# Attention scores in two row tiles of the matmul array, unpadded queries, and a re-ordered opening in a fused attention and feed-forward kernel

## The chip, the cores and the metric

The kernel runs on one core of one Trainium2 chip. The metric is the device time of one execution in microseconds (us), taken as the median of several runs; lower is better. The core has five engines with a queue each that work side by side: PE (matmuls, with its weight loads shown as PEld), DVE (elementwise and reductions), ACT (activation functions and copies), POOL (small copies, and issuing DMAs that change the type) and SP (issuing the other DMAs). They wait for each other through semaphores.

## The reference

Eight batches of eight heads, 576 positions, 64 values a head. Attention sees a window of 32 positions to each side and 8 global positions, which see everything and are seen by all. Its output is the input of a two-layer feed-forward block.

```python
scores = scale * np.matmul(q, k.transpose(0, 1, 3, 2))
mask = np.abs(pos[:, None] - pos[None, :]) <= 32
mask = mask | is_global[:, None] | is_global[None, :]
scores = np.where(mask, scores, -1000000000.0)
scores = scores - np.max(scores, axis=-1, keepdims=True)
attn = np.exp(scores)
attn = attn / (np.sum(attn, axis=-1, keepdims=True) + 1e-09)
x = np.matmul(attn, v)              # to (4608, 512)
h = x @ w_in                        # (4608, 2048)
g = h * np.cos(h)
out = g @ w_out                     # (4608, 512)
```

## The kernel before

**Attention.** Work is cut into 32 pairs of heads (`pr`), four to a batch. For a pair the queries lie in 11 blocks of 56, and each block sees 120 keys of its window and the 8 global ones, 128 in all. The 8 global queries ride along with every block, so that a block has 64 columns (C). Per pair there are these steps:

- `local_k`, `local_q` fill `kw` (keys, two heads of 64 rows stacked on 128 partitions) and `qb` (queries). For the first eight pairs they transpose on PE (`turned`, L492); from then on they copy from `kT`, `qT`, which DMA transposes have filled. `globals_k`, `globals_q` put the global columns in, on POOL.
- `scores(pr, g)` (s): `qb` has a plane for each head in which the other head's 64 rows are zero. One matmul of 128 rows and 128 columns per block then gives both heads side by side. It is called three times a pair, for 4, 4 and 3 blocks; each call has one PSUM bank (tag "s", a ring of three), one exponential on ACT (L527) and one product with the mask on DVE (L528, into `pm`).
- `values(pr)` (p): 22 matmuls of 65 columns (64 values and the row sum) into `pv`, half-width tiles of the array, then sums, reciprocals and the scaled result `xn` on DVE (L542 to L548).
- `turn_x(pr)` (x): six transposes on PE and two DVE operations put `xn` into `xT`; after the last pair of a batch POOL copies the 8 global rows (L568).
- `spread(pr)` (w), for the first eight pairs only: builds `vw`, the values by windows, with 31 small matmuls against shift matrices (L370, L374). Later pairs load `vw` by DMA.

**Feed-forward.** `mlp_in` is a unit of four matmuls of 512 columns (L578), followed by a cosine on ACT (L584) and a product on DVE (L585). The cosine and the exponential need different tables on ACT, so a table load stands at each change. `mlp_out` is a unit of four matmuls of 512 columns (L595); four units fill one output tile, which ACT and DVE copy out in turn and SP stores. There are 144 units of either kind. First-layer units use the PSUM ring "h" (two banks), second-layer units the one bank "o"; while `spare` is on, half of the first-layer units use ring "s".

**Order.** The programmer writes the order by hand, and each engine works through its own part of it strictly in turn. `FRONT` lists the opening, pairs 0 to 7. Then come rounds `s` = 3 to 15. Round 3 (`MID`) has no attention but 18 first-layer units. Each later round has two pairs, called a and z, and follows a string: `1` is a first-layer unit, `2` a second-layer unit, `kc qc kd qd` prepare the next round's pairs, `n` is the sum of squares of `xn` on ACT, `G` issues casts on POOL, `bring` issues transposes and loads on SP. Rounds 4, 5 and 6 have strings of their own (`FOURTH`, `FIFTH`, `SIXTH`). A first-layer unit is only issued when its rows of `xT` are ready; where they are not, the place in the string stays empty. `FIFTH` is the round where only what is left of the first two row tiles can be issued. After the rounds the tail alternates the two kinds of units until all are done.

Of the kernel before, what the change touches and what calls it, by code (L numbers as in the profile page):

```python
# [9 lines left out]
FP32 = mybir.dt.float32  # L10
FP16 = mybir.dt.float16
I32 = mybir.dt.int32
AF = mybir.ActivationFunctionType
# [6 lines left out]
P = 128  # L20
# [24 lines left out]
FOURTH = "2 2 sa0 sa1 sa2 2 sz0 2 sz1 sz2 pa 1 1 2 xa pz G 1 1 2 xz n 1 1 2 kc qc 1 kd qd 2 1"  # L45

FIFTH = "sa0 sa1 sa2 2 2 2 sz0 2 sz1 sz2 pa 1 2 xa pz G 1 2 xz n 1 2 kc qc 1 kd qd 2"

SIXTH = "sa0 sa1 sa2 2 2 2 sz0 2 sz1 sz2 pa 1 1 2 xa pz G 1 1 2 xz n 1 1 D0 2 kc qc D1 1 kd qd D2 2 1"
# [149 lines left out]
def kernel(  # L199
# [138 lines left out]

    def hold(pr):

        nc.gpsimd.tensor_copy(gate, qb[pr % NK][0:1, 0, 0, G : G + 1])

    def vn16(s):
        return xT[:, s, 6 * TT : 9 * TT].rearrange("p (i n) -> p i n", i=NVT)
# [16 lines left out]
    def spread(pr):  # L361

        new, h0 = vn16(pr // 2), 2 * (pr % 2) * D
        for g0 in range(0, NB, 4):
            n = min(4, NB - g0)
            t = ps.tile([P, 4, P], FP32, tag="s", bufs=3)
            for j in range(g0, g0 + n):
                i = j // 2
                parts = ((2, i), (3, i + 1)) if j % 2 else ((0, i), (1, i - 1))
                nc.tensor.matmul(t[:, j - g0], own[:, pr], vg16[:, 0].rearrange("p h d -> p (h d)"), start=True, stop=False)  # L370
                parts = [(a, x) for a, x in parts if x >= 0]
                for a, x in parts:
                    m = min(VT, S - VT * x)
                    nc.tensor.matmul(t[:, j - g0], shift[0:m, a], new[0:m, x, h0 : h0 + 2 * D],  # L374
                                     start=False, stop=(a, x) == parts[-1])
            copy = nc.vector.tensor_copy if g0 == 4 else nc.scalar.copy
            copy(vw[pr % NV][:, g0 : g0 + n, :, 0:D], t[:, 0:n].rearrange("p n (h d) -> p n h d", h=2))

# [4 lines left out]
                view(vg16[(pr % 16) * G : (pr % 16 + 1) * G, pr // 16, h], (0, NB), (1, D)))  # L383


    mask = keep.tile([P, NB, 2, C], FP16)

    def build_mask():

        kid = work.tile([P, NB], FP32, tag="kid", bufs=1)  # L390
        nc.vector.tensor_copy(kid, kid_i)
        gf = work.tile([P, G], FP32, tag="gf", bufs=1)
        nc.vector.tensor_copy(gf, view(gidx_all, (2, G)))
        eq = work.tile([P, NB, G], FP32, tag="eq", bufs=1)
        nc.vector.tensor_tensor(eq, view(kid, (1, NB), (0, G)), view(gf, (0, NB), (1, G)), ALU.is_equal)
        isg = work.tile([P, NB], FP32, tag="isg", bufs=1)
        nc.vector.tensor_reduce(isg, eq, AX.X, ALU.max)
        ge0 = work.tile([P, NB], FP32, tag="ge0", bufs=1)
# [16 lines left out]
        for h in range(2):  # L415
            nc.vector.tensor_tensor(
                mask[:, :, h, G:], view(nk, (1, NB), (0, QB)), view(band[:, G:], (0, NB), (1, QB)), ALU.mult)
            nc.vector.tensor_scalar(
                mask[:, :, h, 0:G], view(val, (1, NB), (0, G)), own[:, 0:1], None, ALU.mult)
# [11 lines left out]
        for h in range(2):  # L431
            nc.vector.tensor_copy(mask[0:G, :, h, G:], view(one, (0, NB), (0, QB)))


    qgT = keep.tile([P, B * NP, G], FP16)
# [44 lines left out]

    def globals_q(pr):
        qp = qb[pr % NK]
        nc.gpsimd.tensor_copy(qp[0:D, 0, :, 0:G], view(qgT[0:D, pr], (0, NB), (1, G)))
        nc.gpsimd.tensor_copy(qp[D:P, 1, :, 0:G], view(qgT[D:P, pr], (0, NB), (1, G)))

    def turned(src, pr, n):

# [14 lines left out]
            nc.vector.tensor_copy(to, view(kT[pr // 2 % 2][:, pr % 2], (QB, NB), (1, W)))  # L502

    def local_q(pr):
        if pr < 2 * HY:
            t = turned(qn[pr // 2 % 2], pr, QP)
        for h in range(2):
            hp = slice(h * D, (h + 1) * D)
            to = qb[pr % NK][hp, h, :, G:]
            if pr < 2 * HY:  # L510
                copy = nc.scalar.copy if h == 0 or pr == 1 else nc.vector.tensor_copy
                copy(view(to, (C, NB), (RW, QB // RW), (1, RW)),  # L512
                     view(t[hp], (QB // RW, NB), (1, QB // RW), (QP, RW)))
            else:
                nc.vector.tensor_copy(to, view(qT[pr // 2 % 2][hp, pr % 2], (QB, NB), (1, QB)))  # L515

    def scores(pr, g):
        kp, qp = kw[pr % NK], qb[pr % NK]
        if g == 0:
            pm_of[pr] = work.tile([P, NB, 2, C], FP16, tag="pm", name="pm")  # L520
        pm = pm_of[pr]
        g0, n = 4 * g, min(4, NB - 4 * g)
        st = ps.tile([P, 4, P], FP32, tag="s", bufs=3)
        for j in range(n):
            nc.tensor.matmul(st[:, j], kp[:, g0 + j], view(qp[:, :, g0 + j], (NB * C, 2), (1, C)), start=True, stop=True)  # L525
        e = work.tile([P, 4, P], FP16, tag="e", bufs=3)
        nc.scalar.activation(e[:, :n], st[:, :n], AF.Exp, scale=scale)  # L527
        nc.vector.tensor_tensor(  # L528
            view(pm[:, g0], (1, n * P)), view(e, (1, n * P)), view(mask[:, g0], (1, n * P)), ALU.mult)

    def values(pr):
        pm, vp = pm_of.pop(pr), vw[pr % NV]
        for j in range(NB):
            for h in range(2):
                r0 = (j % 2) * C
                c0 = ((j // 2) % 3) * 130 + h * 65
                nc.tensor.matmul(pv[r0 : r0 + C, j // 6, c0 : c0 + 65], pm[:, j, h], vp[:, j, h],  # L537
                                 start=True, stop=True)
        den = pv[:, :, D : D + 1]
        rp = r_all[:, pr]  # L540
        dg = work.tile([G, 2], FP32, tag="dg")
# [10 lines left out]
    def turn_x(pr):  # L552
# [142 lines left out]
    with tc.manual_schedule():  # L695
# [14 lines left out]
        gather(k, kg32, 0)  # L710
        gather(q, qg32, 0)
        gather(v, vg32, 0)
        for t in (kn[1], qn[1], qb[2], qb[3]):
            nc.scalar.memzero(t.rearrange("p a b c -> p (a b c)"))
        load_qk(1)
        for i in range(2):
            nc.vector.memset(qb[i], 0.0)
        build_shifts()
        for i in range(NV):
            nc.vector.memset(vw[i][:, :, :, D : D + 1], 1.0)  # L720
# [53 lines left out]
                 "w": spread, "C": cast_vn, "V": lambda _: hold(9), "A": later_rows, "D": later_globals, "O": load_w_out, "K": lambda s: cast_half(s, "kq" if s == 4 else "vkq"), "B": bring, "m": lambda _: one(False), "t": lambda _: mlp_act()}  # L774
        ready[0] = 1
        for step in FRONT.split():
            f = (STEPS | OTHER)[step[0]]
            f(*[int(x) for x in (step[1:] or "0").split(".")])
        ready[0], front[0] = 2, False
# [85 lines left out]
```

## Time and profile before

| | us |
|---|---|
| median of 3 runs (367.13, 369.73, 370.02) | 369.73 |
| profiled execution | 371.58 |
| its span, first instruction to last | 369.8 |
| opening (`FRONT`), up to the first matmul of MID | 0 to 71.65 |
| MID, 18 first-layer units | 71.65 to 87.78 |
| rounds 4 to 15 | 87.78 to about 291 |
| tail | about 291 to 369.8 |

Costs of single operations, from the groups by line: exponential of 512 columns 596 ns, of 384 columns 492; mask product 427 and 361; cosine 687; product g 685; query copy on DVE 460 (a 64-partition plane, two to a pair), on ACT 667 and 803 on DVE in the opening; sum of squares 1476; table load 1283.

How to read it: a timeline row gives start, length, engine, line, operation and tiles, and how many like instructions were merged; what stands in brackets is the idle time before and what ended it. Matmuls overlap, and the end of each is modelled, so the time of one is read from start to start. "Issue" in the chain of waits is time in which the engine waited for nothing that the profile shows.

### The profile page before, as it was taken

What the parts mean: (1) busy time and instruction counts of PE and PEld (TensorE: products, weight loads), DVE (VectorE), ACT (ScalarE), POOL (GpSimd) and SP (SyncE); (2) the same over time, 40 slices, a digit from 0 to 9 for tenths busy, and PEclk for the clock granted to TensorE, in tenths of its full rate; (3) what the DMA queues carried; (4) which work ended last, traced back from release to release, by engine and by line L of the source; (5) the groups of instructions that cost most, each with busy time, mean ns of one, the idle gap of its engine ahead of it and who ended that gap; (6) DMA issues with size and microseconds to landing.
All of it is one profiled execution on the core that took longest, in us unless ns stands there. A gap on an engine that the chain in (4) does not pass through costs nothing.

```text
span 369.8 us, 8014 instructions
## 1 busy us (share of the span) xinstructions
PE 335.9 (91%) x2934; PEld 184.9 (50%) x2934; DVE 266.3 (72%) x615; ACT 249.5 (67%) x384; POOL 105.9 (29%) x239
## 2 busy tenths in 40 slices
PE   0399883999998999999999999999999999999992
PEld 0277673545553545555555555555555444444441
DVE  7659974696888888888888888888878445455410
ACT  5488882679776677778777868677787756644300
POOL 6735670161335250705253252603000100000000
PEclk9999997899999999999999999999999999999999
DMA  5979999999999999999999999999920000100111
GB/s 92 197 129 159 180 165 107 198 176 147 102 161 105 194 126 195 125 169 138 195 161 159 160 142 165 160 202 118 130 59 31 28 30 28 57 30 28 53 64 65
DMA packets 176280, 45.57 MB, mean 123 GB/s; under 512 B 164937, under 2 KB 171337, under 8 KB 176041
## 3 DMA queue, kind: packets, MB, share of 16 engines
q1 hardware_dynamic: 112601, 27.61, 58.3%
q0 software_dynamic: 63632, 17.37, 50.3%
q8 instruction: 25, 0.41, 0.5%
q14 instruction: 22, 0.18, 0.2%
HBM read 45.07 MB, written 20.05 MB: 176 GB/s over the span
## 4 chain that ended last, share of the span: by engine, by line
PE 79%; DVE 6%; issue 5%; ACT 3%; POOL 3%; DMA 2%; POOLq 0%; ACTq 0%
PE po L595 32%; PE ph L578 30%; PE st L525 5%; PE pv L537 4%; PE tx L560 2%; PE t L374 2%; DMA qn<-in_q_dram 2%; DVE g L585 2%; ACT e L527 1%; PE t L370 1%; PE t L492 1%; PE pn L628 1%; DVE xn L548 1%; POOL q L262 1%; ACT qb L512 1%
## 5 line engine op out<-in xcount | busy, mean ns | idle before, releaser
L584 ACT ACTIVATE cos<-ph,pio 128x512 f16<-128x512 f32 x144 | 97.1, 687 | 66.3 <-PE ph L578 64.7
L595 PE MATMUL po<-w_out,g 128*128 128x512 f16 x576 | 141.6, 379 | 0.0
L578 PE MATMUL ph<-xT,w_in 128*128 128x512 f16 x576 | 140.1, 379 | 0.3 <-DVE g L585 0.2
L585 DVE TENSOR_TENSOR g<-cos,ph 128x512 f16<-128x512 f16 x144 | 95.9, 685 | 46.9 <-ACT cos L584 44.9
L595 PEld LDWEIGHTS <-g 128*128 128x128 f16 x576 | 55.2, 98 | 62.1
L578 PEld LDWEIGHTS <-w_in 128*128 128x128 f16 x576 | 53.6, 98 | 60.5 <-issue 1.3
L527 ACT ACTIVATE e<-st 128x512 f16<-128x512 f32 (+1 forms) x96 | 47.9, 561 | 15.5 <-PE st L525 9.4
L528 DVE TENSOR_TENSOR pm<-e,mask 128x512 f16<-128x512 f16 (+1 forms) x96 | 37.2, 405 | 22.8 <-ACT e L527 21.0
L752 POOL COPY gate<-xn 1x1 f16<-1x1 f16 x12 | 2.2, 181 | 132.3 <-DVE xn L548 132.3
L525 PE MATMUL st<-qb,kw 128*128 128x128 f16 x352 | 29.2, 223 | 9.4 <-issue 5.0
L525 PEld LDWEIGHTS <-kw 128*128 128x128 f16 x352 | 24.1, 100 | 19.8 <-issue 9.1
L548 DVE TENSOR_TENSOR xn<-pv,r_all 128x768 f16<-128x768 f32 x32 | 30.7, 958 | 1.7
L568 POOL COPY xT<-xg 128x4 f16 x64 | 19.6, 306 | 28.7 <-DVE xT L563 25.3
L262 POOL DMA_DIRECT2D q<-in_q_dram x12 | 26.2, 2181 | 0.0
L614 ACT ACTIVATE sq<-xn 128x1536 f16<-128x1536 f16 x16 | 23.6, 1476 | 0.0
L515 DVE COPY qb<-qT 64x616 f16<-64x616 f16 x48 | 22.1, 460 | 0.3
L374 PE MATMUL t<-xT 112*128 112x128 f16 (+1 forms) x168 | 21.1, 240 | 0.7 <-ACT xT L349 0.4
L600 ACT COPY o<-po 128x512 f32<-128x512 f32 x18 | 10.5, 586 | 15.5 <-PE po L595 15.1
L262 POOL DMA_DIRECT2D k<-in_k_dram x12 | 19.8, 1646 | 0.0
L370 PE MATMUL t<-vg,xT 128*128 128x128 f16 x88 | 18.4, 242 | 0.9 <-issue 0.6
L537 PE MATMUL pv<-vw,pm 128*64 128x65 f16 x704 | 18.5, 199 | 0.0
L602 DVE COPY o<-po 128x512 f32<-128x512 f32 x18 | 12.3, 685 | 6.9 <-PE po L595 6.9
(123 smaller groups left out, 326.8 us busy)
## 6 DMA issues: line engine op xcount, KB each, us to landing
out_dram<-o SPq DMA_DIRECT2D x36, 256.0 KB
vw<-v SPq DMA_DIRECT2D x35, 165.0 KB
v<-in_v_dram POOLq DMA_DIRECT2D x12, 288.0 KB, 4.3
k<-in_k_dram POOLq DMA_DIRECT2D x12, 288.0 KB, 9.2
q<-in_q_dram POOLq DMA_DIRECT2D x12, 288.0 KB, 15.8
vn<-in_v_dram SPq DMA_DIRECT2D x20, 112.0 KB
w_in<-in_moe_w_in_dram POOLq DMA_DIRECT2D x4, 512.0 KB, 12.3
w_out<-in_moe_w_out_dram POOLq DMA_DIRECT2D x1, 2048.0 KB
```

What stands on the lines that cost most here:

```text
L262: nc.gpsimd.dma_start(dst[s].rearrange("t (h d) -> t h d", h=4), dview(src, base, (D, S), (S * D, 4), (1, D)))
L374: nc.tensor.matmul(t[:, j - g0], shift[0:m, a], new[0:m, x, h0 : h0 + 2 * D], start=False, stop=(a, x) == parts[-1])
L525: nc.tensor.matmul(st[:, j], kp[:, g0 + j], view(qp[:, :, g0 + j], (NB * C, 2), (1, C)), start=True, stop=True)
L527: nc.scalar.activation(e[:, :n], st[:, :n], AF.Exp, scale=scale)
L528: nc.vector.tensor_tensor(view(pm[:, g0], (1, n * P)), view(e, (1, n * P)), view(mask[:, g0], (1, n * P)), ALU.mult)
L537: nc.tensor.matmul(pv[r0 : r0 + C, j // 6, c0 : c0 + 65], pm[:, j, h], vp[:, j, h], start=True, stop=True)
L548: nc.vector.tensor_tensor(view(xn, (384, 2), (D, 6), (1, D)), view(pv, (512, 2), (65, 6), (1, D)), view(rp, (6, 2), (1, 6), (0, D)), ALU.mult)
L578: nc.tensor.matmul(ph, w_in16[:, j, f * P : (f + 1) * P], xT[:, j, t * TT : (t + 1) * TT], start=(j == 0), stop=(j == NC - 1))
L584: nc.scalar.activation(cos, ph, AF.Sin, bias=pio2)
L585: nc.vector.tensor_tensor(g, cos, ph, ALU.mult)
L595: nc.tensor.matmul(po, g16[:, f, s * P : (s + 1) * P], w_out16[:, f], start=(f == 0), stop=(f == NF - 1))
L614: nc.scalar.activation(sq, view(xn, (1, 2 * BP * P)), AF.Square, accum_out=x_sq[:, s : s + 1])
```

## The change

- `qb` loses its planes: both heads lie in one tile of 128 partitions without zeros. `local_q` is one copy, and in the opening it is on DVE for even pairs and on ACT for odd ones; `globals_q` is one copy. The clearing of `qb` goes, and the mask is kept once instead of per head.
- `scores(pr)` is one call. Each block has two matmuls, one per head, on 64 rows of the array; each head writes its own PSUM banks. Four banks are used at a time: three of ring "s", and one of "o" in the opening or of "h" in the rounds. Exponentials are two of 512 columns and two of 192; mask products are two of 512 columns and one of 384.
- `values` issues its matmuls so that the column halves alternate.
- `spread` merges neighbouring matmuls: 16 instead of 31 a pair.
- `turn_x` always uses ring "s".
- The orders: in a round the two score calls stand whole, with four second-layer units between them (`FOURTH`: two ahead and two between); eight second-layer units a round as before. In `FRONT` values and transposes come one stage later, four first-layer units are issued instead of two, with the spare banks on, and the second sum of squares closes it.

```diff
-ORDER = "sa0 sa1 sa2 2 2 2 sz0 2 sz1 sz2 pa 1 1 2 xa pz G 1 1 2 xz n 1 1 2 kc qc 1 kd qd 2 1"
+ORDER = "sa 2 2 2 2 sz pa 1 1 2 xa pz G 1 1 2 xz n 1 1 2 kc qc 1 kd qd 2 1"
...
-FIFTH = "sa0 sa1 sa2 2 2 2 sz0 2 sz1 sz2 pa 1 2 xa pz G 1 2 xz n 1 2 kc qc 1 kd qd 2"
+FIFTH = "sa 2 2 2 2 sz pa 1 2 xa pz G 1 2 xz n 1 2 kc qc 1 kd qd 2"
...
-FRONT = ("s0.0 s0.1 s0.2 k1 q1 C0 w0 s1.0 s1.1 s1.2 L2 p0 k2 q2 C1 w1 x0 s2.0 s2.1 s2.2 W0 p1 k3 q3 C2 w2 x1 "
-         "s3.0 s3.1 s3.2 L3 W1 A g4 g5 p2 k4 q4 w3 x2 s4.0 s4.1 s4.2 g6 g7 c4 K4 W2 W3 p3 k5 q5 C3 w4 x3 s5.0 s5.1 s5.2 p4 k6 q6 w5 x4 n0 "
-         "s6.0 s6.1 s6.2 K5 p5 k7 q7 w6 x5 B4 s7.0 s7.1 s7.2 O p6 w7 n1 x6 m p7 m x7 t t")
+FRONT = ("s0 k1 q1 C0 w0 s1 L2 k2 q2 C1 w1 p0 s2 W0 k3 q3 x0 C2 w2 p1 s3 L3 W1 A g4 g5 k4 q4 x1 w3 p2 "
+         "s4 g6 g7 c4 K4 W2 W3 k5 q5 x2 C3 w4 p3 s5 k6 q6 x3 w5 p4 s6 K5 k7 q7 x4 w6 p5 s7 B4 O w7 x5 n0 p6 + m m x6 p7 t t m m x7 t t n1 -")
...
-    qb = [keep.tile([P, 2, NB, C], FP16, name=f"qb{i}") for i in range(NK)]
+    qb = [keep.tile([P, NB, C], FP16, name=f"qb{i}") for i in range(NK)]
...
+            nc.tensor.matmul(view(t, (1, n * P)), own[:, pr], view(vg16[:, 0].rearrange("p h d -> p (h d)"), (0, n), (1, P)),
+                             start=True, stop=False, skip_group_check=True)
+            for a, j, k, x in runs:
+                m = min(VT, S - VT * x)
+                nc.tensor.matmul(view(t[:, j], (2 * P, k), (1, P)), shift[0:m, a], new[0:m, x : x + k, h0 : h0 + 2 * D],
+                                 start=False, stop=(a, j, k, x) == runs[-1], skip_group_check=True)
...
-    def scores(pr, g):
...
-        for j in range(n):
-            nc.tensor.matmul(st[:, j], kp[:, g0 + j], view(qp[:, :, g0 + j], (NB * C, 2), (1, C)), start=True, stop=True)
...
+    def scores(pr):
+        kp, qp = kw[pr % NK], qb[pr % NK]
+        pm = pm_of[pr] = work.tile([P, 2, NB, C], FP16, tag="pm", name="pm")
+        tags = (("s", 3), ("s", 3), ("s", 3), ("o", 1) if front[0] else ("h", 2))
+        st = [ps.tile([P, 512], FP32, tag=tag, bufs=bufs, name="st") for tag, bufs in tags]
+        for j in range(NB):
+            for h in range(2):
+                hp = slice(h * D, (h + 1) * D)
+                nc.tensor.matmul(st[j // 8 * 2 + h][:, j % 8 * C : j % 8 * C + C], kp[hp, j], qp[hp, j], start=True, stop=True)
         for h in range(2):
+            e = work.tile([P, 512], FP16, tag="e", bufs=3)
+            nc.scalar.activation(e, st[h], AF.Exp, scale=scale)
+            nc.vector.tensor_tensor(view(pm[:, h], (1, 512)), e, view(mask, (1, 512)), ALU.mult)
+        e = work.tile([P, 512], FP16, tag="e", bufs=3)
+        n = (NB - 8) * C
+        for h in range(2):
+            nc.scalar.activation(e[:, h * n : (h + 1) * n], st[2 + h][:, 0:n], AF.Exp, scale=scale)
+        nc.vector.tensor_tensor(view(pm[:, 0, 8], (NB * C, 2), (1, n)), view(e, (n, 2), (1, n)), view(mask[:, 8], (0, 2), (1, n)), ALU.mult)
...
-        for j in range(NB):
+        for j0 in range(0, NB, 2):
             for h in range(2):
...
+                for j in range(j0, min(j0 + 2, NB)):
...
-        tx = ps.tile([P, BP, P], FP16, tag="o" if front[0] else "s", bufs=1 if front[0] else 3)
+        tx = ps.tile([P, BP, P], FP16, tag="s", bufs=3)
...
-        for t in (kn[1], qn[1], qb[2], qb[3]):
+        for t in (kn[1], qn[1]):
...
-        for i in range(2):
-            nc.vector.memset(qb[i], 0.0)
```

More of the change, by code (lines that the diff above doesn't have):

```diff
@@ L366, in spread @@
             t = ps.tile([P, 4, P], FP32, tag="s", bufs=3)
[L367 to L375, printed above, removed]
+            runs = []
+            for first, a, back in ((0, 0, 0), (0, 1, 1), (1, 2, 0), (1, 3, -1)):
+                js = [j for j in range(g0 + first, g0 + n, 2) if j // 2 - back >= 0]
+                full = [j for j in js if j // 2 - back < NVT - 1]
+                runs += [(a, x[0] - g0, len(x), x[0] // 2 - back) for x in (full, js[len(full) :]) if x]
+            nc.tensor.matmul(view(t, (1, n * P)), own[:, pr], view(vg16[:, 0].rearrange("p h d -> p (h d)"), (0, n), (1, P)),
[4 more added lines that the diff above has]
+                                 start=False, stop=(a, j, k, x) == runs[-1], skip_group_check=True)
             copy = nc.vector.tensor_copy if g0 == 4 else nc.scalar.copy
@@ L383, in load_vg @@
                 view(vg16[(pr % 16) * G : (pr % 16 + 1) * G, pr // 16, h], (0, NB), (1, D)))
-    mask = keep.tile([P, NB, 2, C], FP16)
+    mask = keep.tile([P, NB, C], FP16)
     def build_mask():
@@ L414, in build_mask @@
         nc.vector.memset(own[0:G], 0.0)
[L415 to L419, printed above, removed]
+        nc.vector.tensor_tensor(
+            mask[:, :, G:], view(nk, (1, NB), (0, QB)), view(band[:, G:], (0, NB), (1, QB)), ALU.mult)
+        nc.vector.tensor_scalar(
+            mask[:, :, 0:G], view(val, (1, NB), (0, G)), own[:, 0:1], None, ALU.mult)
         gc = work.tile([G, 1], FP32, tag="gc", bufs=1)
@@ L430, in build_mask @@
         nc.vector.tensor_scalar(one, one, 0.5, None, ALU.is_le)
-        for h in range(2):
-            nc.vector.tensor_copy(mask[0:G, :, h, G:], view(one, (0, NB), (0, QB)))
+        nc.vector.tensor_copy(mask[0:G, :, G:], view(one, (0, NB), (0, QB)))
     qgT = keep.tile([P, B * NP, G], FP16)
@@ L504, in local_q @@
     def local_q(pr):
+        to = qb[pr % NK][:, :, G:]
         if pr < 2 * HY:
             t = turned(qn[pr // 2 % 2], pr, QP)
-        for h in range(2):
[L508 to L515, printed above, removed]
@@ L517, in scores @@
-    def scores(pr, g):
[L518 to L523, printed above, removed]
-        for j in range(n):
[L525 to L529, printed above, removed]
+            copy = nc.scalar.copy if pr % 2 else nc.vector.tensor_copy
@@ L531, in values @@
     def values(pr):
         pm, vp = pm_of.pop(pr), vw[pr % NV]
-        for j in range(NB):
+        for j0 in range(0, NB, 2):
             for h in range(2):
[L535 to L538, printed above, removed]
+                for j in range(j0, min(j0 + 2, NB)):
+                    r0 = (j % 2) * C
+                    c0 = ((j // 2) % 3) * 130 + h * 65
+                    nc.tensor.matmul(pv[r0 : r0 + C, j // 6, c0 : c0 + 65], pm[:, h, j], vp[:, j, h],
+                                     start=True, stop=True)
@@ L776 @@
         for step in FRONT.split():
+            if step in "+-":
+                spare[0] = step == "+"
+                continue
+            if step in "+-":
+                spare[0] = step == "+"
+                continue
             f = (STEPS | OTHER)[step[0]]
```

13 lines of the change are left out of this document (8 added, 5 removed).

## The prediction

> **What bounds it now.** I read the page first, then busy time by stage, then one late round engine by engine, then the opening and its chain of waits.
>
> ```profile
> PE 335.9 (91%) x2934; PEld 184.9 (50%) x2934; DVE 266.3 (72%) x615; ACT 249.5 (67%) x384; POOL 105.9 (29%) x239
> ```
>
> PE is busy 91%. By stage (columns: stretch, length, busy time of PE, weight loads, DVE, ACT, POOL, granted clock, DMA share, GB/s):
>
> ```profile
> 52.20:62.30 10.10, 4.02 (x84) 3.29 (x78) 4.54 (x11) 4.45 (x9) 1.72 (x2) 0.93 1.51 92
> 62.30:72.40 10.10, 9.43 (x108) 6.88 (x108) 5.86 (x17) 6.42 (x10) 0.00 (x0) 0.74 1.68 185
> 72.40:87.90 15.50, 15.27 (x71) 6.74 (x69) 13.82 (x26) 12.57 (x20) 8.62 (x24) 1.00 1.65 167
> 138.66:155.58 16.92, 16.92 (x143) 9.07 (x142) 14.22 (x33) 12.92 (x20) 6.19 (x14) 1.00 1.66 160
> ```
>
> So three regimes: an opening to 71.6 us with PE waiting; the block MID, 18 first-layer units one after the other; then rounds of 16.92 us in which PE has no gap while DVE idles 2.7 us and ACT 4.0 us. One round on PE:
>
> ```profile
> 154.80 0.78 PE L525 MATMUL st<-qb,kw 128*128 128x128 f16 x11
> 155.41 2.75 PE L595 MATMUL po<-w_out,g 128*128 128x512 f16 x12
> 158.00 0.39 PE L525 MATMUL st<-qb,kw 128*128 128x128 f16 x4
> 158.23 1.03 PE L595 MATMUL po<-w_out,g 128*128 128x512 f16 x4
> 159.09 0.55 PE L525 MATMUL st<-qb,kw 128*128 128x128 f16 x7
> 159.57 0.57 PE L537 MATMUL pv<-vw,pm 128*64 128x65 f16 x22
> 160.07 1.90 PE L578 MATMUL ph<-xT,w_in 128*128 128x512 f16 x8
> ```
>
> Read start to start: 11 score matmuls 0.61 us (55.5 ns each), a unit of four 512-column matmuls 0.864, seven scores ahead of the values 0.48 where 0.39 is due: going over to half-width tiles costs 0.09. The 22 value matmuls take 0.50, about 0.41 without the way back, so 18.6 ns each.
>
> ACT and DVE in the same round:
>
> ```profile
> 157.00 2.02 ACT L527 ACTIVATE e<-st 128x512 f16<-128x512 f32 x4
> 159.51 0.98 ACT L527 ACTIVATE e<-st 128x512 f16<-128x512 f32 x2 [0.49 <-DVE pm L528]
> 160.51 1.28 ACT L584 ACT_TABLE_LOAD   x1
> 161.80 1.27 ACT L584 ACTIVATE cos<-ph,pio 128x512 f16<-128x512 f32 x2
> ```
> ```profile
> 161.44 0.96 DVE L548 TENSOR_TENSOR xn<-pv,r_all 128x768 f16<-128x768 f32 x1
> 162.53 1.28 DVE L585 TENSOR_TENSOR g<-cos,ph 128x512 f16<-128x512 f16 x2
> ...
> 165.68 1.28 DVE L585 TENSOR_TENSOR g<-cos,ph 128x512 f16<-128x512 f16 x2
> ```
>
> ACT works strictly in turn: exponentials, table load, cosines; DVE follows it with pm, xn, then the products g.
>
> **The rounds.** Count from the first score matmul (154.80 = 0). Before: exponentials end at 5.69, the cosine table is loaded by 7.0, the first g starts on DVE at 7.73, xn of the first pair ends at 7.60, PE starts its transposes at 7.88, the fifth first-layer unit at 11.74 only 0.18 after the g (third of the round) that frees its bank. PE sets the pace with 0.2 to 0.3 us to spare.
>
> After, a score call is 22 matmuls of 64 rows and 64 columns, the heads alternating. No row shows row tiles. Nearest: the transposes of keys, which alternate between two column halves:
>
> ```profile
> 35.70 0.50 PE L492 MATMUL t<-ident,kn 86*64 86x86 f16 x16
> 36.00 0.48 PE L492 MATMUL t<-ident,qn 78*64 78x78 f16 x16
> ```
>
> 16 in 0.30 us, 18.8 ns each. Call the pace p. Low end: half the columns at today's speed, two at a time, 13.9 ns; high end: no overlap and weight loads of 128 columns as dear as a whole matmul now, 55.5. I take 18.8. A call is then 0.09 in + 22p (0.41) + 0.09 out = 0.59 against 0.61: no gain. The second call goes on into the values, whose 0.09 is paid already. Values in the new order: 0 to 0.1 saved, taken as 0, since 18.6 is the alternating pace already.
>
> But the order changes: sa, four second-layer units, sz, where sa and sz were split and z's first bank came before the fourth. The first bank of z is written at 0.59 + 4x0.864 + 0.09 + 16p (0.30) = 4.43, its exponential starts 0.2 later (as a cosine does behind a unit: 154.80, 155.00): 4.63. Four exponentials instead of three: 512 columns step 0.50; from 596 ns (512) and 490 (384) I take 336 for 192, stepping 0.24: 0.50+0.50+0.24+0.34 = 1.58, end 6.21. Waiting behind them on ACT are the table load and the cosines: first g at 6.21+1.29+0.69+0.04 = 8.23, 0.50 later than before. On DVE pm, sums and xn follow (0.05+0.36+1.45+0.06): transposes at 8.13, 0.25 later. DVE's run from the first g to the third is 3.83 us (7.73 to 11.56), so the fifth unit starts at 8.23+3.83+0.07 = 12.13 instead of 11.74; 0.38 a round. The fourth score bank shares the ring of the first-layer units, so unit two also waits for z's last exponential (6.2 against 6.0); that lies inside the same delay. 11 whole rounds: +4.2 us. With p = 13.9 it is 38x4.9 ns less a round (22 matmuls of sa and 16 of sz): +2.1. With 27.8: +7.9.
>
> [...]
>
> The query copies shrink by one 0.47 us copy per pair, POOL's by one: hidden, because DVE and POOL idle at the end of a round; if DVE were full they would be worth 0.9 a round.
>
> Round FIFTH has no first-layer units left after the opening took two more: four become two, -1.73. Before it took 15.7, with 1.35 us of wait in it. After: transposes 8.1, values 0.9, two units 1.7, xn of the second pair ends about 10.9, two units, scores at 13.1 or, by the DVE queue (key copy took 1.6 there instead of 0.53), 14.2. Taken 13.7: -2.0.
>
> **The opening.** Before: scores of pair 0 at 16.72, pair 1 at 23.89, pair 7 at 56.92 (5.5 us a pair), MID at 71.65. There DVE works without a gap (one pair 30.04 to 35.34). After:
> - Pair 0: one ACT query copy (0.67) leaves the path to the global keys, and DVE is rid of 2.9 us (memsets 1.38, doubled mask work 1.56). I take -0.9; pair 1 also loses one copy of 0.67: scores at 22.8.
> - Values and transposes come a stage later, so a stage is no longer scores-to-xn but the longer of two queues. ACT from score start: exponentials to 2.0, keys 1.17, queries 0.57 (odd pairs), cast 0.52, first spread bank 0.48 = 4.74. DVE: pm to 2.4, query 0.83 (even), transposes 0.5, cast 0.8, spread 0.61 = 4.3 to 5.1. 4.4 to 4.9 a stage, six stages 28.5. Merged spread matmuls (31 to 16) stream the same columns: nothing gained on PE, which is not last here. Transposes now take a score bank, so the third spread bank waits for DVE's copy of them, to 3.7; that lies inside the stage.
> - PE also stops for its own instructions:
>
> ```profile
> 57.25 5.04 issue
> ```
>
> (chain of waits). Such stops, at 41.36, 48.73 and 57.25, lie 256 PE instructions apart, and 1.5 us before each ends a 16 KB packet of the instruction queue lands. A pair had 204 instructions, now 196: the same stops remain, 1.5 us to pair 7, which then starts at 52.8 (-4.1).
> - Behind it: scores 0.6, spread 1.9, three transposes 1.2, two value calls 1.0, four first-layer units 3.45 = 8.2, plus the long stop. It may fall to 0 or reach 6.5; 3 taken. It also cost the clock (0.74 above). MID at 64.0, against 71.65: -7.7, ends -2.5 and -11. MID itself is the same 18 units. The second sum of squares (1.68 on ACT) now stands ahead of MID's first cosine: PE has five banks to run ahead in, so it costs nothing, 0.4 if a bank is short. bring(4), moved behind pair 7's scores, stands on SP behind row loads that end at 47 either way.
>
> **Sum.** -7.7 - 2.0 + 4.2 = -5.5. The profiled run took 371.58 (span 369.8); that gives 366.1. The median of the runs is 1.85 lower, 369.73, so 364.2; I say 364. About 1% (3.7 us) is what a measurement can tell.
>
> **Rivals.**
> 1. The two heads do not overlap. For: no row has weight loads of 128 columns under 55.5 ns. Against: column halves overlap. At 27.8 ns (one after the other): +7.9 - 9.7 = -1.8, 368; chance 0.16. At 55.5: 11x1.77 = +19.5, total +9.8, 379.5, slower; it turns to a loss against now from p = 32; chance 0.14. [...]
> 2. The opening gains only 2 us: instruction stops of 6 us behind pair 7, or w_out (issued 51.68, its queue drains until about 78) holding the first second-layer unit. Sum +0.2, 370; chance 0.16. DMA's share is over 1.5 there; against: 92 GB/s from 52 to 62 shows room.
> 3. ACT and DVE have more slack than counted, rounds stay PE's: about 16.6 us, -3.3 for 11, total -13, 357; chance 0.10.
> 4. Forecast: 0.44.
>
> Faster by over 1% (below 366): 0.42 of case 4, all of 3, 0.02 of the first rival: 0.54. Within 1%: the rest of 4, most of 27.8 ns and of rival 2: 0.28. Slower: 0.14 and the bad end of rival 2: 0.18. Range 356 to 374: from rival 3 to past rival 2; it leaves out the far end of rival 1.
>
> **What would show it.** In a late round: score calls of 0.5 to 0.6 us start to start, z's exponentials ending near 6.2, PE idle 0.2 to 0.5 before the first transposes and before the fifth unit, rounds near 17.3. Pair 7's scores near 53, MID near 64, FIFTH near 13.7. Wrong if rounds fall under 16.9, if a score call exceeds 0.8, or if MID starts after 69.

## The result and the profile after

| | before | after |
|---|---|---|
| median of 4 runs, same chip (us) | 369.01 (367.13 to 370.02) | 363.68 (362.89 to 364.17) |
| profiled execution, span | 371.58, 369.8 | 362.89, 361.2 |
| pair 7's scores | 56.92 | 52.74 |
| MID | 71.65 to 87.78 | 62.33 to 78.77 |
| FIFTH, SIXTH | 15.73, 17.45 | 12.85, 17.98 |
| late round | 16.92 | 17.14 |

The ratio of the medians is 0.9861, 95% interval 0.9819 to 0.9904. The kernel before scatters much more than this one: in the three later jobs its 19 to 23 runs lay between 364.5 and 376.1, with medians of 369.39, 368.93 and 369.86. A ratio leaves out the slow runs, those over 1.5% above the fastest of their kernel, while the medians hold all runs, so the two need not agree to the last per mille. The medians above differ by 5.3 us and the two profiled executions by 8.7: the profiled execution before lies 2.6 above its median, the one after 0.8 below.

The page's row of PE, and busy time by stage (columns as before: stretch, length, PE, weight loads, DVE, ACT, POOL, granted clock, DMA share, GB/s):

```profile
PE 333.4 (92%) x3158; PEld 168.3 (47%) x3158; DVE 252.3 (70%) x583; ACT 246.4 (68%) x409; POOL 94.0 (26%) x207
```
```profile
28.47:48.04 19.57, 17.52 (x397) 12.85 (x394) 17.02 (x46) 16.57 (x33) 10.36 (x21) 1.00 1.35 169
53.17:62.33 9.16, 8.24 (x100) 4.81 (x95) 7.36 (x20) 7.22 (x12) 0.81 (x1) 1.00 1.73 116
62.33:78.77 16.44, 15.95 (x72) 7.01 (x72) 14.10 (x26) 14.40 (x22) 7.19 (x20) 1.00 1.55 197
161.55:178.69 17.14, 17.05 (x165) 8.38 (x165) 13.95 (x32) 13.05 (x21) 5.20 (x10) 1.00 1.60 156
```

The first row holds four pairs of the opening; in the profile before, the same four took 22.17:

```profile
28.76:50.93 22.17, 19.18 (x413) 16.17 (x414) 20.76 (x51) 17.99 (x31) 15.00 (x31) 1.00 1.38 176
```

That one stretch flatters the change: in before_again the same four pairs took 20.90 and in before_pad64 20.46. All six stages from pair 1 to pair 7 took 33.03 here, 33.93 and 32.53 in these two, and 29.99 in the changed kernel.

The second row of the changed kernel answers to the two rows with clocks of 0.93 and 0.74 before: from pair 7 to MID there is no stop of 5 us, and the clock stays at 1.00. The last row is a late round, 0.22 longer than before. That round on PE:

```profile
161.55 0.49 PE L520 MATMUL st<-qb,kw 64*128 64x64 f16 x22
161.97 3.63 PE L596 MATMUL po<-w_out,g 128*128 128x512 f16 x16
165.53 0.49 PE L520 MATMUL st<-qb,kw 64*128 64x64 f16 x22
165.96 0.56 PE L538 MATMUL pv<-vw,pm 128*64 128x65 f16 x22
166.46 2.12 PE L579 MATMUL ph<-xT,w_in 128*128 128x512 f16 x8
168.42 1.03 PE L596 MATMUL po<-w_out,g 128*128 128x512 f16 x4
169.47 0.51 PE L561 MATMUL tx<-ident,xn 128*128 128x128 f16 x6
...
173.42 1.89 PE L579 MATMUL ph<-xT,w_in 128*128 128x512 f16 x8
```

Read start to start. A score call takes 0.42 to 0.43 (161.55 to 161.97, 165.53 to 165.96); 0.43 less 0.09 for the change of tile sizes (an estimate from the rows before, 0.48 less 0.39) is 15.5 ns a matmul. The first two first-layer units take 1.96 where 1.73 is due: 0.23 of wait. The second-layer unit behind them (0.86) would let the transposes start at 169.28; they start at 169.47, 0.19 late. ACT and DVE in the same round show what they wait for:

```profile
165.97 1.09 ACT L523 ACTIVATE e<-st 128x512 f16<-128x512 f32 x2 [0.79 <-PE st L520]
166.94 0.56 ACT L528 ACTIVATE e<-st 128x192 f16<-128x192 f32 x2
167.53 1.28 ACT L585 ACT_TABLE_LOAD   x1
168.82 1.26 ACT L585 ACTIVATE cos<-ph,pio 128x512 f16<-128x512 f32 x2
```
```profile
168.46 0.96 DVE L549 TENSOR_TENSOR xn<-pv,r_all 128x768 f16<-128x768 f32 x1
169.54 1.28 DVE L586 TENSOR_TENSOR g<-cos,ph 128x512 f16<-128x512 f16 x2
```

ACT stands idle for 0.79 until z's scores come, behind the fourth second-layer unit; xn of the first pair starts at 6.91 of the round and the first g at 7.99, where before it was 6.64 and 7.73. So the delay that the prediction's chain expects is there, at about half its size (0.26 for g where 0.50 was worked out), and it passes on to the transposes and the unit behind them.

### The profile page after: what moved, and what is told of

Read it like the earlier page. It is cut to its first block, busy times and chain, and to the rows that moved or that the text cites. A ratio compares the mean times of both kernels' runs of the same rounds, so it can differ in the third digit from the quotient of the medians.

```text
span 361.2 us, 8418 instructions
## 1 busy us (share of the span) xinstructions
PE 333.4 (92%) x3158; PEld 168.3 (47%) x3158; DVE 252.3 (70%) x583; ACT 246.4 (68%) x409; POOL 94.0 (26%) x207
## 4 chain that ended last, share of the span: by engine, by line
PE 75%; ACT 8%; DMA 5%; DVE 5%; issue 4%; POOL 1%; SPq 0%; ACTq 0%; POOLq 0%
PE po L596 33%; PE ph L579 28%; PE tx L561 3%; PE t L375 3%; PE st L520 3%; ACT e L523 3%; PE pv L538 3%; DMA vw<-vg 2%; DMA kn<-in_k_dram 2%; DVE xn L549 2%; ACT e L528 2%; DVE g L586 2%; DMA vg<-in_v_dram,gidx_rows 1%; PE t L371 1%; ACT sq L615 1%
## 5 line engine op out<-in xcount | busy, mean ns | idle before, releaser
L579 PE MATMUL ph<-xT,w_in 128*128 128x512 f16 x576 | 141.6, 379 | 1.3 <-DVE g L586 0.4
L596 PE MATMUL po<-w_out,g 128*128 128x512 f16 x576 | 139.7, 380 | 0.2 <-ACT o L601 0.2
L523 ACT ACTIVATE e<-st 128x512 f16<-128x512 f32 x64 | 34.7, 594 | 11.7 <-PE st L520 11.2
L524 DVE TENSOR_TENSOR pm<-e,mask 128x512 f16<-128x512 f16 x64 | 26.6, 424 | 22.9 <-ACT e L523 21.4
L561 PE MATMUL tx<-ident,xn 128*128 128x128 f16 x192 | 16.2, 220 | 3.7 <-DVE xn L549 3.4
L520 PEld LDWEIGHTS <-kw 64*128 64x128 f16 x704 | 12.9, 97 | 11.6 <-issue 9.1
L561 PEld LDWEIGHTS <-xn 128*128 128x128 f16 x192 | 11.7, 98 | 14.1 <-DVE xn L549 11.8
L375 PE MATMUL t<-xT 112*128 112x256 f16 (+2 forms) x104 | 17.3, 274 | 0.9 <-DVE xT L347 0.9
L528 ACT ACTIVATE e<-st 128x192 f16<-128x192 f32 x64 | 18.0, 345 | 0.0
```

Source lines behind the costliest of these rows:

```text
L375: nc.tensor.matmul(view(t[:, j], (2 * P, k), (1, P)), shift[0:m, a], new[0:m, x : x + k, h0 : h0 + 2 * D], start=False, stop=(a, j, k, x) ...
L523: nc.scalar.activation(e, st[h], AF.Exp, scale=scale)
L524: nc.vector.tensor_tensor(view(pm[:, h], (1, 512)), e, view(mask, (1, 512)), ALU.mult)
L579: nc.tensor.matmul(ph, w_in16[:, j, f * P : (f + 1) * P], xT[:, j, t * TT : (t + 1) * TT], start=(j == 0), stop=(j == NC - 1))
L596: nc.tensor.matmul(po, g16[:, f, s * P : (s + 1) * P], w_out16[:, f], start=(f == 0), stop=(f == NF - 1))
```

## The experiments

Two theories had to be tested. **For the opening**: the new order of the pairs' steps, together with the smaller copies, shortens the path to MID; the rival is that the gain is merely the loss of the long stop there, which may hang on the count of PE's instructions ahead of it. **For the rounds**: the 0.22 us come from the late start of z's exponentials; the rival is PE's own work. All ratios are to the kernel before, run in the same job.

**The kernel before, once more.** No edit.

> The kernel before, unchanged, profiled once more: does its long stop of PE in the opening (5.04 us, ending 62.3 us) have the same size in every execution? If the stop is an instruction fetch that is held up in the DMA queues, its place (the same matmul of pair 7's scores) stays and its size varies by some us, and the span with it: 365 to 370. If it is a wait for data of pair 7, place and size stay within 0.5 us and the span is 369 to 370.

370.76, and the same stop, on the chain of waits:

```profile
58.33 3.23 issue
```

It stands in front of the same instruction, the fourth score matmul of pair 7, in both executions, but took 5.04 in the one and 3.23 here. A stop in a fixed place with a length that changes would make the runs scatter. Two of the 19 runs of this kernel in that job came to 364.48 and 365.17 us, with a mean granted clock of 0.999 and 0.997 where the other 17 have 0.984 to 0.996; this fits runs with little or no stop, but neither was profiled.

**The blocks of PE's instructions moved.**

```diff
+        for _ in range(2):
+            idle = ps.tile([P, 512], FP32, tag="h", bufs=2)
+            for _ in range(32):
+                nc.tensor.matmul(idle[:, 0:16], ident16, ident16[:, 0:16], start=True, stop=True)
```

> The kernel before with 64 small matmuls of 16 columns ahead of everything on PE, where it idles until 8.7 us, so that all later instructions stand 128 places (64 matmuls and 64 weight loads) further on. Fetch theory: the long stop moves 128 PE instructions earlier in the program, from the fourth score matmul of pair 7 to the key or query transposes of pair 7, and as the fetch is then asked for some 3 us sooner, ahead of the DMA transposes of 48 us, it shrinks to 0 to 2 us: 3 to 6 us less than the kernel before in the profile, 1 to 5 in the times. Data theory: the stop stays at pair 7's scores with 5 us, times unchanged.

364.61 (364.01 to 365.22), ratio 0.9877 [0.9812, 0.9942]. There is no long stop, and the stretch from pair 7's scores to MID is

```profile
56.51:64.85 8.34, 7.11 (x107) 4.86 (x108) 6.26 (x17) 6.52 (x10) 0.00 (x0) 1.00 1.70 114
```

8.34 us at clock 1.00, against 14.73 before (56.92 to 71.65). Of these 6.4 us, 5.04 are the stop; the other 1.35 lie outside it, and behind it the clock was lower (0.71 from 62.29 to 71.65). Rounds are unchanged at 16.92. So 64 useless matmuls make the kernel before about as fast as the changed one (ratios 0.9877 and 0.9861): the stop, with the clock behind it, is worth what the change gained. That the stop goes when the count of instructions ahead of it changes is shown. In the first profile a 16 KB packet of the instruction queue moves from 58.35 to 60.71, while PE stands, which suggests a fetch of instructions; the profile does not show what PE waits for. The two stops ahead of it in that profile, 256 PE instructions apart like this one, are short (0.96 us up to 42.32 and 0.59 up to 49.33); this one took 5.04, and 3.23 in before_again.

**The new forms with the old order of the opening.** `FRONT` as before, with whole score calls.

```diff
-FRONT = ("s0 k1 q1 C0 w0 s1 L2 k2 q2 C1 w1 p0 s2 W0 k3 q3 x0 C2 w2 p1 s3 L3 W1 A g4 g5 k4 q4 x1 w3 p2 "
-         "s4 g6 g7 c4 K4 W2 W3 k5 q5 x2 C3 w4 p3 s5 k6 q6 x3 w5 p4 s6 K5 k7 q7 x4 w6 p5 s7 B4 O w7 x5 n0 p6 + m m x6 p7 t t m m x7 t t n1 -")
+FRONT = ("s0 k1 q1 C0 w0 s1 L2 p0 k2 q2 C1 w1 x0 s2 W0 p1 k3 q3 C2 w2 x1 "
+         "s3 L3 W1 A g4 g5 p2 k4 q4 w3 x2 s4 g6 g7 c4 K4 W2 W3 p3 k5 q5 C3 w4 x3 s5 p4 k6 q6 w5 x4 n0 "
+         "s6 K5 p5 k7 q7 w6 x5 B4 s7 O p6 w7 n1 x6 m p7 m x7 t t")
```

> The changed kernel with the opening's old order (values and transposes in their old place, two first-layer units, no spare banks). Order theory: six stages take 32 to 33 us again instead of 30.0 and four first-layer units are left for FIFTH; MID starts 2 to 5 us later than 62.3 although it has 1.7 us less in front of it, FIFTH is 2.9 us longer: 5 to 8 us slower than the changed kernel, about level with the kernel before. Theory of cheaper steps (one query copy, merged spread matmuls, no clearing): the opening is as fast per stage as now, 30 us, and the kernel loses 1 to 2 us at most against the changed one.

371.92 (368.81 to 373.7), ratio 1.0073 [1.0031, 1.0114]. The six stages from pair 1 to pair 7 take 5.78 us each (22.88 to 57.57) where the changed kernel has 5.00, the long stop is back, now at the values of pair 7,

```profile
62.82 0.38 PE L539 MATMUL pv<-vw,pm 128*64 128x65 f16 x6 [4.15 <-issue]
```

and MID starts at 70.61. FIFTH is 15.85 again, since only two first-layer units ran in the opening. This is worse than either theory had it: stages and MID's start both come later than the first one said. Less the stop of 4.15, MID would start at 66.5, no earlier than in before_pad64 (64.85), and the late rounds are at 17.15. The new forms alone make the kernel no faster, and by the ratio 0.7% slower.

**The old forms with the new order.** The kernel before with the new `FRONT` and its `+` and `-`, scores in three calls.

> The kernel before with the new opening's order (values and transposes a stage later, four first-layer units with spare banks) and nothing else of the change. Order theory: MID starts 3 to 6 us earlier than 71.6, FIFTH shrinks by 2 to 3 us, rounds stay at 16.92: 360 to 364 us, faster than the changed kernel's 363.7 by up to 3. Theory of cheaper steps: MID starts at 70 to 72, only FIFTH's 1.7 us are gained: 367 to 369.

370.4 (368.31 to 371.12), ratio 1.0083 [1.0039, 1.0126]: both expectations missed, by 6.4 us and by 1.4. MID does start earlier, at 67.56, without a long stop, with stages of 5.59 us (5.51 before, 5.42 in before_pad64: they are no shorter). But MID waits 1.61 for one product g (76.36), the next round is no shorter than before (15.73) though two units have left it, and the one behind it takes 19.04. At the end of FIFTH, on POOL, DVE and PE:

```profile
112.83 0.50 POOL L257 DMA_DIRECT2D v<-in_v_dram  x1
113.32 1.64 POOL L261 DMA_DIRECT2D k<-in_k_dram  x1
114.39 2.18 POOL L261 DMA_DIRECT2D q<-in_q_dram  x1
115.47 3.42 POOL L567 COPY xT<-xg 128x4 f16 x8
```
```profile
113.64 3.29 DVE L501 COPY kw<-kT 128x1320 f16<-128x1320 f16 x1
116.86 0.93 DVE L514 COPY qb<-qT 64x616 f16<-64x616 f16 x2
```
```profile
117.89 1.33 PE L524 MATMUL st<-qb,kw 128*128 128x128 f16 x11 [3.07 <-POOL xT L567]
119.01 3.84 PE L594 MATMUL po<-w_out,g 128*128 128x512 f16 x12
```

POOL issues the requests for a later round; beside them DVE's copy of K takes 3.29 where it takes 0.53 elsewhere, and POOL's own copies come last. PE waits 3.07, and then the scores take 1.12 instead of 0.61 (granted clock 0.50 from 117.89 to 119.01) and the three units 3.68 instead of 2.59 (0.70 up to 122.69).

**Those requests later.**

```diff
-FIFTH = "sa0 sa1 sa2 2 2 2 sz0 2 sz1 sz2 pa 1 2 xa pz G 1 2 xz n 1 2 kc qc 1 kd qd 2"
+FIFTH = "sa0 sa1 sa2 2 2 2 sz0 2 sz1 sz2 pa 1 2 xa pz G 1 2 xz n 1 2 kc qc 1 kd qd 2 K8"
...
-                if s == n - 3:
+                if s == n - 3 and s != 5:
                     cast_half(n, "vkq")
```

> The kernel before with the new opening's order (370.4), and in its round FIFTH the requests of V, K and Q (three DMA instructions that GpSimd issues, 0.50, 1.64 and 2.18 us) placed behind the copies of K and Q instead of ahead of them. Theory (while GpSimd issues them, VectorE's copy of K takes 3.29 us and not 0.53, GpSimd's own eight copies for xT come last, and the next scores wait 3.07 us for them; TensorE then runs the scores and three units at a lower clock): the K copy takes 0.53, the wait falls to 0.3 to 1.0, FIFTH from 15.73 to 13.0 to 13.7, SIXTH from 19.04 to 17.5 to 18.0, and the time to about 366. Rival (the wait is for something else, the transposed K and Q themselves): FIFTH stays at 15.7 and the time at 370.

368.17 (365.86 to 371.47), ratio 0.9983 [0.994, 1.0026], 2.2 less than without this edit in another job, and 1% less by the ratios; about 366 was expected. On DVE and PE, in the profiled execution, the longest of the ten at 371.47, whose MID started 2.2 late:

```profile
115.81 0.53 DVE L501 COPY kw<-kT 128x1320 f16<-128x1320 f16 x1
```
```profile
117.29 0.77 PE L524 MATMUL st<-qb,kw 128*128 128x128 f16 x11 [0.30 <-POOL xT L567]
...
140.81 0.82 PE L536 MATMUL pv<-vw,pm 128*64 128x65 f16 x22 [1.23 <-DMA vw<-vg]
```

The copy is at 0.53, the wait at 0.30, FIFTH at 12.95 and SIXTH at 17.45: 4.4 us gained in these two rounds, and the theory holds for the wait. But the two rounds behind took 19.15 and 17.77 instead of 16.92, with PE waiting for values (1.23 at 140.81), which gives 3.1 back in that execution. That the later requests are the cause of it is likely and was not tested. The changed kernel has the same collision, but there only the second pair's copy of K is caught; the first pair's K and Q copies have just got through, and PE starts its scores at 108.86 without a wait:

```profile
107.75 0.53 DVE L500 COPY kw<-kT 128x1320 f16<-128x1320 f16 x1
108.19 0.46 DVE L510 COPY qb<-qT 128x616 f16<-128x616 f16 x1
108.57 2.77 DVE L500 COPY kw<-kT 128x1320 f16<-128x1320 f16 x1
```

**Two heads in one row tile after the other.** The two loops of a score call exchanged.

```diff
-        for j in range(NB):
-            for h in range(2):
+        for h in range(2):
+            for j in range(NB):
```

> The changed kernel with the two loops of a score call exchanged: first the eleven matmuls of head 0, all in the upper row tile, then the eleven of head 1 in the lower. Overlap theory (two neighbouring matmuls in different row tiles run beside each other, which is why 22 of them take 0.43 from start to start): nothing overlaps any more but at the seam, a call takes 0.6 to 0.7, a round 17.3 to 17.6, and the time is 366 to 369. Rival (a call is bound by the rate at which instructions are issued, about 19 ns each, tiles or not): a call stays at 0.43, a round at 17.14, the time at 363.7.

366.86 (364.31 to 369.72), ratio 0.9967 [0.9917, 1.0016]. Rounds 17.36. A call on PE:

```profile
163.70 0.71 PE L520 MATMUL st<-qb,kw 64*128 64x64 f16 x22
164.35 3.63 PE L596 MATMUL po<-w_out,g 128*128 128x512 f16 x16
```

0.65 instead of 0.43: less the same 0.09, 25.5 ns a matmul within one row tile against 15.5 when neighbours lie in different tiles. So the overlap is real, and worth 0.22 a call; the round, with two calls, grows by 0.22 and not by 0.44, and why was not followed up.

**The blocks moved in the changed kernel.** The same 64 matmuls as above.

> The changed kernel with 64 matmuls of 16 columns ahead of TensorE's work, which move the boundaries between the 16 KB blocks of its instructions by 128 instructions, as they did in the kernel before. Fetch theory (the long stop of the kernel before falls on a block whose fetch is asked for in the slow stretch of the DMA queues, 50 to 62 us; the changed kernel has none because its block was fetched at 50.1): a fetch now falls at about 54 to 56 us, a stop of 1 to 4 us comes up there, the middle round starts 1 to 5 us later, 364.5 to 368. Rival (the changed opening loads the queues less, so that no fetch is late wherever it falls): no stop, 363.7 within 0.5.

365.16 (364.44 to 366.25), ratio 0.994 [0.9912, 0.9967]. No long stop: no wait of PE from pair 1 to MID exceeds 0.7. MID started at 64.66, 2.3 later than in the first profile, but pair 0's scores started 2.0 later too (17.73 against 15.70). That delay is the padding's own: PE was still at the idle matmuls at 12.20, and the first key transposes started at 13.58 instead of 8.73. So the 365.16, 1 us above what the rival expected, is no price of a stop. On the stop the rival was right: the new opening has no long stop, with the idle matmuls or without.

**The 2 MB load of the second layer's weights later.** `O` moved in the kernel before.

```diff
-         "s6.0 s6.1 s6.2 K5 p5 k7 q7 w6 x5 B4 s7.0 s7.1 s7.2 O p6 w7 n1 x6 m p7 m x7 t t")
+         "s6.0 s6.1 s6.2 K5 p5 k7 q7 w6 x5 B4 s7.0 s7.1 s7.2 p6 w7 n1 x6 m p7 m x7 O t t")
```

> The kernel before with the 2 MB load of the second layer's weights asked for at the end of the opening instead of ahead of its last three pairs' values. If this load is what holds up the instruction fetch at 58.35 us: the fetch takes about 1 us, the stop of 3 to 5 us at pair 7's scores goes, the middle round starts at 65 to 67 instead of 71.2 and the time is 364 to 366. If the stretch is slow for another reason (the transposing transfers of K and Q, issued from 49 to 58 us): the stop stays at 2 to 5 us, the middle round starts at 69 to 72, the time is 368 to 371. In both the weights must land by 87 us; if they do not, the first second-layer unit waits, which would show as its start behind 88.

376.87 (375.09 to 378.39), ratio 1.0237 [1.0169, 1.0305]. PE's timeline, and its waits near MID's end:

```profile
61.37 1.01 PE L525 MATMUL st<-qb,kw 128*128 128x128 f16 x8 [3.34 <-issue]
```
```profile
PE po L595 <- DMA w_out<-in_moe_w_out_dram: 5.4, 1, 5.4
```

The stop stays, so that load does not cause it, though at 2 MB it was the largest transfer asked for just then. The load itself came too late: the first second-layer unit waited 5.4 and started at 92.05. Note the packet of the instruction queue here: it moved from 57.98 to 58.86, and PE went on at 61.37, 2.5 us behind its end. In the first profile it moved from 58.35 to 60.71, and PE went on at 62.29, 1.6 behind. Here the packet itself took 0.88, no longer than the four ahead of it in the first profile (0.88 to 1.28), and the stop is 3.34 all the same; so a slow transfer of the packet is not the whole of the stop. What makes these stops long in the old opening stays open.

**z's scores one unit earlier.** In the changed kernel, all four strings:

```diff
-ORDER = "sa 2 2 2 2 sz pa 1 1 2 xa pz G 1 1 2 xz n 1 1 2 kc qc 1 kd qd 2 1"
+ORDER = "sa 2 2 2 sz 2 pa 1 1 2 xa pz G 1 1 2 xz n 1 1 2 kc qc 1 kd qd 2 1"
...
-FOURTH = "2 2 sa 2 2 sz pa 1 1 2 xa pz G 1 1 2 xz n 1 1 2 kc qc 1 kd qd 2 1"
+FOURTH = "2 2 sa 2 sz 2 pa 1 1 2 xa pz G 1 1 2 xz n 1 1 2 kc qc 1 kd qd 2 1"
```

> The changed kernel with block pair z's scores one second-layer unit earlier (after three of the four units, not after four). Delay theory (the 0.22 us that a round gained comes from z's exponentials, which start behind the fourth unit and push ACT's table load, the cosine and VectorE's normalizations back, so that xa starts at 7.92 and the fifth unit, the transposes and unit two wait 0.49 in all): z's scores end 0.86 earlier, xa starts near 7.8 or a little before, the waits shrink to some 0.27, a round comes to about 16.93, and eleven rounds make it about 2.3 us faster than the changed kernel, about 361.4. Rival (the 0.22 is TensorE's own work, 22 score matmuls a call and four mode changes, whatever their place): the round stays at 17.14 or gets longer by a mode change, 363.7 to 364.7.

360.93 (360.02 to 362.09), ratio 0.9819 [0.9773, 0.9865]. A round is 16.90:

```profile
161.51 0.49 PE L520 MATMUL st<-qb,kw 64*128 64x64 f16 x22
161.94 2.76 PE L596 MATMUL po<-w_out,g 128*128 128x512 f16 x12
164.64 0.60 PE L520 MATMUL st<-qb,kw 64*128 64x64 f16 x22
165.17 1.04 PE L596 MATMUL po<-w_out,g 128*128 128x512 f16 x4
166.14 0.57 PE L538 MATMUL pv<-vw,pm 128*64 128x65 f16 x22
166.64 1.90 PE L579 MATMUL ph<-xT,w_in 128*128 128x512 f16 x8
168.38 1.03 PE L596 MATMUL po<-w_out,g 128*128 128x512 f16 x4
169.27 0.51 PE L561 MATMUL tx<-ident,xn 128*128 128x128 f16 x6
```

The first two first-layer units take 1.74 (166.64 to 168.38), so unit two no longer waits; the transposes start at 7.76 of the round instead of 7.92. z's call takes 0.53 and not 0.43. It starts at 164.64, and a's second exponential of 512 columns ends at 164.70 (163.62 plus 1.08), so the 0.1 is most likely a wait for a score bank; the rows name no releaser.

**And one more unit earlier.** `sa 2 2 sz 2 2 pa` in the same place, `2 2 sa sz 2 2 pa` in FOURTH.

> The changed kernel with z's scores behind two of the four units (in FOURTH directly behind a's). In the run with three they waited 0.11 us for a score bank; the banks come free with a's exponentials, 2.7 to 3.6 us into the round. If that holds, z's call, due at 2.2 us, cannot end before the last of three shared banks is free, about 3.4: it holds TensorE up by 0.7 to 1.0 us a round, nothing behind it gets earlier, a round comes to 17.5 to 17.8, the time to 367 to 371. If the banks are no limit and only the place of the exponentials counts: 16.8 to 16.9 and 360 to 361.

369.71 (369.09 to 371.14), ratio 1.0051 [0.9999, 1.0104]; rounds of 17.73:

```profile
164.37 0.49 PE L520 MATMUL st<-qb,kw 64*128 64x64 f16 x22
164.80 1.90 PE L596 MATMUL po<-w_out,g 128*128 128x512 f16 x8
167.21 0.19 PE L520 MATMUL st<-qb,kw 64*128 64x64 f16 x1 [0.52 <-ACT e L523]
167.61 0.49 PE L520 MATMUL st<-qb,kw 64*128 64x64 f16 x21 [0.21 <-ACT e L523]
```

PE waits for the banks that a's exponentials still hold. Behind four units z's scores come too late for ACT, behind two too early for the banks.

**The changed kernel and the version with three units on one chip.**

> The changed kernel as it is, on the same chip as the next run, so that the two can be compared: 363 to 365, rounds of 17.14, no stop of more than 1.5 us in the opening.

> The changed kernel with z's scores behind three units, on the same chip as the run before: rounds of 16.90, and by eleven times 0.24 and the 0.3 to 0.4 us of rounds FOURTH to SIXTH 2.6 to 3.6 us faster than that run. If its lead came from a lucky opening alone: 0 to 1 us.

363.62 (362.39 to 365.17) and 360.79 (359.99 to 362.31), six runs each, and the two ranges do not overlap: 2.8 us, or 0.8%. Rounds are 17.14 and 16.90. In the profiled executions MID starts at 63.56 and 63.22, so 0.3 of the difference is the opening's.

## Why the prediction was right, point by point

The time (364.0 against 363.68) came out, but that is in part luck. In the profiled executions the terms add up to -9.3 for the opening, -2.9 for FIFTH and +3.6 for MID and the other rounds, -8.6 in all, where -5.5 was worked out. The median moved by only 5.3, because the profiled execution before was a long one for its kernel and the one after a short one. The directions of the three terms were right; their sizes, and what the opening's gain is made of, were so in part.

- **A score call.** Taken at 18.8 ns a matmul; measured 15.5, and 25.5 with the heads apart (heads_apart). The first rival, heads that do not overlap, falls.
- **The rounds.** Taken +0.38 each, measured +0.22. With 15.5 ns in place of 18.8 the same chain gives 17.17, against 17.14. Each step of it is in the rows: z's exponentials end at 5.95 of the round (6.21 predicted), the first g starts at 7.99 (8.23), the transposes at 7.92 (8.13), the fifth first-layer unit at 11.87 (12.13). The waits, 0.23 at unit two, 0.19 at the transposes and 0.07 more before the fifth unit, make 0.49; PE's own work is then 16.65, 0.27 less than before. That sum is what the third rival expected as a round, 16.6, but its slack did not exist: ACT and DVE were needed in time, and were late. That their delay comes from the place of z's scores is shown by moving it: one unit earlier gives 16.90; two units earlier gives 17.73, where PE waits for score banks instead.
- **FIFTH.** Taken -2.0, measured -2.9: its K copy was not caught by the requests, so that the lower of the two ends for its scores held. SIXTH and the round behind it gave 1.2 back (17.98 and 17.56, where before they took 17.45 and 16.92), the latter with 0.23 of wait for values; the prediction counted them like the other rounds.
- **The opening.** Taken -7.7, measured -9.3 (71.65 to 62.33). Pair 7 came at 52.74 for 52.8, but by errors that cancel: the six stages took 30.0 and not 28.5, and the 1.5 us of shorter stops did not come, since PE's timeline lists no issue stop between pair 1 and pair 7. The 0.9 taken for pair 0 also came in this execution alone: its scores start at 15.70 here, at 16.73 to 16.86 in the other five unpadded executions of the new opening, and at 16.60 to 16.80 in five of the six with the old forms (17.75 in the sixth). In the five others with the new opening pair 7 is at 53.63 to 54.26. The mis-sized term is behind pair 7: "plus the long stop. It may fall to 0 or reach 6.5; 3 taken", on the ground that "the same stops remain". It fell to 0, in every profiled execution of the changed kernel. The work from pair 7 to MID took 9.6 where 8.2 was worked out, so the error in MID's start is 1.7 and not 3.
- **What the gain consists of.** Here the prediction was wrong in weight. It laid the gain on the shorter path of the opening; before_pad64 shows that the kernel before gains as much by losing its stop alone (ratio 0.9877 [0.9812, 0.9942], against 0.9861 and, in after_again, 0.9881 [0.9815, 0.9947] for the changed kernel). Against that run's profile, MID starts 2.5 earlier in the first profile of the changed kernel, 1.2 to 1.6 earlier in after_again, z_again, z_after_three and z_after_two (63.22 to 63.64), which have the same opening, 1.0 earlier in heads_apart, and 0.2 earlier in after_pad64; two first-layer units more are done by then. What FIFTH saves with these is given back by the rounds: from FOURTH's first scores to the last second-layer matmul the two kernels need 273.4 (before_pad64) and 273.6. So with the stop set aside the change as predicted is worth at most some 1 us (364.61 against 363.6 to 363.7, from different jobs), and by the ratios nothing that can be told from zero. What can be told is the further step, z's scores after three units: 2.8 us on one chip.
- **Order and forms.** The prediction added their savings. The runs show that each alone makes the kernel slower by under 1% (1.0073 and 1.0083), and both together faster: stages of 5.78 and 5.59 us alone, 5.0 to 5.1 together, where the kernel before has 5.42 to 5.66. With the old order the new forms keep the stop, and their scores wait for DVE's xT (0.23 and 0.30); what else makes their stages long was not tested. With the new order the old forms keep PE's greater work (19.1 us in four pairs, 17.5 with the new forms) and meet the collision of K copies and requests.
- **The second rival**, an opening that gains only 2, falls with MID at 62.33 to 63.85 in the unpadded executions.

The best version is the changed kernel with z's scores behind three units: 360.79 to 360.93, ratios to the kernel before 0.9804 [0.974, 0.9869] and 0.9819.

## What to carry to other kernels

Before costing a change to a stage that has a stop with no releaser in it, ask whether the stop belongs to the work or to the count of instructions ahead of it: here 64 idle matmuls in front, 128 instructions, took it away and showed what the stage is worth without it (8.34 us from pair 7's scores to MID, 14.73 with it). Check that the idle instructions do not themselves hold up the start, as they did in after_pad64. When an engine that "has slack" works strictly in turn, follow the chain in time and not its idle share: here 0.9 us in the place of one score call decides between 16.90, 17.14 and 17.73. And test an order only together with the forms that it was written for: the parts of this change lose alone what they gain together.

## What the runs showed of the hardware that was not expected

- PE stops with no releaser in the profile, at the same instruction in three profiled executions (before, before_again, before_late_wout), for 5.04, 3.23 and 3.34 us, and for 4.15 at another place with the new forms in the old order. From the stop's end to MID, 7.8 to 9.6 us, the mean granted clock is then 0.69 to 0.78. In the first profile this is 0.50 from 60.81 to 67.64 and 1.00 from 67.64 to 71.65. With 128 instructions more in front, the stop is gone (before_pad64: clock 1.00 from 56.51 to 64.85).
- 22 matmuls of 64 rows and 64 columns that alternate between two row tiles take 0.43 us from start to start (after), 11 in one row tile and then 11 in the other 0.65 (heads_apart). Less 0.09 for the change of tile sizes, an estimate, that is 15.5 and 25.5 ns each.
- A copy of 1320 columns on DVE took 0.53 us with POOL's requests behind it (bno_late_gather) and 3.29 while POOL issued them (before_new_opening); in the changed kernel 0.53 and 2.77.
